# Windowed attention and a gated convolution: band masks by TensorE, gates from SBUF, and a new order

## The chip, the cores and the metric

The kernel runs on one core of a Trainium2 chip. The metric is the device time of one execution in microseconds. Five engines work side by side, each on its own list of instructions in order: TensorE (PE, matmuls, with its weight loads shown as PEld), VectorE (DVE), ScalarE (ACT), GpSimd (POOL), and SyncE (SP), which here does nothing but issue DMAs. The engines wait for each other through semaphores. SBUF is the working memory of 128 partitions; PSUM, eight banks of 128 x 512 float32, takes the results of TensorE.

## The reference

Inputs are q, k, v of shape (8 batches, 8 heads, 576 positions, 64), w_in (512 x 1024), conv_w (3 x 1024) and w_out (1024 x 512), all float32.

```python
scores = np.matmul(q, k.transpose(0, 1, 3, 2)) / np.sqrt(64)
mask = np.abs(pos[:, None] - pos[None, :]) <= 32
attn = softmax(np.where(mask, scores, -1e9))
x = (attn @ v), heads side by side      # (8, 576, 512)
h = np.maximum(x @ w_in, 0.0)           # (8, 576, 1024)
conv = conv_w[0]*h[s-1] + conv_w[1]*h[s] + conv_w[2]*h[s+1]   # along the sequence
out = (h * sigmoid(conv)) @ w_out       # (8, 576, 512)
```

Every query sees only the keys at most 32 positions away, so the attention is a band.

## The kernel before

The program is written out as one list of words, ORDER, some 1,100 steps long. Each word is a step on one engine (`sc,2,1,0@0` is the score block of batch 2, head group 1, part 0, into PSUM bank 0), and every engine runs its instructions in the order in which the words stand. The list was made by a planner that isn't part of the kernel; at run time nothing is decided. Pinned (L159) wraps the engines, so that every instruction shows the one line L165 in the profile and is told apart by its tiles.

**Attention.** A unit is a batch and a group of four heads, 16 units in all. `lq`, `lk` load q and k of a unit into `st` (589,824 bytes each as a whole, or by halves), `cq`, `ck` cast them to bf16 (`qb`) on ACT (a) or POOL (p), `tq`, `tk` transpose 32 x 32 blocks on DVE into `qT`, `kT`. `sc` (L247) makes a score block: for each of four or five tiles of 64 queries it multiplies 128 keys by 64 queries, for four heads, in two halves of the head dimension; the array is used as four row tiles of 32 rows, one head's half each, and each head writes its own PSUM bank. `ex` is the exponential on ACT from PSUM into `attn`. `mk` (L273) multiplies `attn` by a mask on DVE (d), or cuts the two triangles off with two selects on POOL (p). `av` multiplies by v with a column of ones, `nr` divides by the sum into `xn`. v is loaded by `lv` (five blocks of 128 positions a batch, into the single tile `vst`), cast by `cv` into `ve`, and copied shifted by 64 partitions into `vo` by `vo` or by a DMA, `vd`. `xn` is turned into `xT` by a DMA (`xt`) or by TensorE and a copy (`xp`, `xe`).

**The gated convolution.** Two batches make three chunks of 384 positions, twelve chunks in all. The first two are worked as halves of 192, so there are 14 pieces P; 0 to 3 are halves. Each piece has four channel pairs (2 x 128 channels). For each pair: `ph` is the projection, eight matmuls; `re` the relu into `hT` on ACT; `pc` (L448) the convolution into PSUM; `th` (L498) the tanh (the sigmoid is written with it); `ga` (L515) the gate on DVE, (tanh + 1) x h into `gT`; later `py` is the output product, `ye` its copy out of PSUM and `st` the store. The convolution has kinds, chosen word by word:

- P: three matmuls by diagonal matrices for each 128 channels, on the full array.
- D, A: the same on quarters, 64 x 64 tiles, four at a time; the second half of the result then stands with its partitions swapped. Kind D gates with three instructions, the last two over 64 partitions; kind A has its second tanh, in two instructions, put the partitions right and write to `z` in SBUF.
- X: the first tap on ACT, the other two on DVE (`tp`), in PSUM.
- G: all taps on POOL in SBUF (`zg`), tanh from there into PSUM.

All other kinds gate from PSUM. `conv_w` itself is loaded by ACT's queue (`s1`, L607), turned by a matmul (`cw`), copied out (`cc`) and spread into diagonals (`dg`, on ACT or DVE). `id` and `ia` are matmuls whose results nobody reads; they keep TensorE running at the start.

## Time and profile before

| | |
|---|---|
| median of three runs | 211.1 us (210.82 to 212.81) |
| the profiled execution | 212.45 us |
| its span, first to last instruction | 210.7 us |
| TensorE's mean granted clock | 0.992 |
| POOL busy | 147.7 us, 177 instructions |
| DMA traffic | 46.9 MB, 223 GB/s in the mean |
| last output product ends | 207.76 us after the span's start |

The profile lists busy time by engine, by stretches of the span, by groups of equal instructions, and the chain of work that ended last. "Idle before" of a group is the time its engine stood still just ahead of it, and the names behind an arrow tell what ended that wait. Where two instructions of an engine overlap by some tenths, their mean durations add up to more than the busy time.

### The profile page before, as it was taken

The numbers are of one execution on the slowest core, as the hardware profiler recorded it, in microseconds if no ns is written. First come the engines' busy times: TensorE is split into PE (matmuls) and PEld (weight loads), VectorE is DVE, ScalarE is ACT, GpSimd is POOL, SyncE is SP. The second block draws the span as 40 slices with busy tenths as digits, with TensorE's granted clock in tenths as the row PEclk, the third lists the DMA queues.
The fourth block names the chain that finished last, engine by engine and source line by source line (L and its number), as shares of the span: only waits on it lengthen the run. The fifth ranks groups of instructions, "written<-read, shape, count | busy, mean of one in ns | idle before, by whom it ended". The sixth has DMA issues, their size and how long they took to land.

```text
span 210.7 us, 7141 instructions
## 1 busy us (share of the span) xinstructions
PE 195.7 (93%) x2951; PEld 113.9 (54%) x2974; DVE 178.4 (85%) x297; ACT 172.7 (82%) x265; POOL 147.7 (70%) x177
## 2 busy tenths in 40 slices
PE   3867999999999799999999999999999999999994
PEld 2233798895465345654464554554545565555443
DVE  4677977999999998797999779899999587899860
ACT  2986798997999798779999699899978799759911
POOL 2650586499999469999699998539954879955700
PEclk9979999999999999999999999999999999999999
DMA  5999999999998895899999999999976444222225
GB/s 176 325 213 347 388 220 273 366 296 272 318 279 194 195 319 151 267 292 238 241 258 176 226 252 231 262 297 245 290 144 165 99 142 128 46 71 103 100 100 199
DMA packets 66165, 46.90 MB, mean 223 GB/s; under 512 B 53180, under 2 KB 55508, under 8 KB 66132
## 3 DMA queue, kind: packets, MB, share of 16 engines
q1 hardware_dynamic: 66096, 46.43, 84.0%
q8 instruction: 23, 0.38, 0.8%
q14 instruction: 10, 0.08, 0.1%
q10 hardware_dynamic: 36, 0.01, 0.1%
HBM read 32.52 MB, written 9.44 MB: 199 GB/s over the span
## 4 chain that ended last, share of the span: by engine, by line
PE 56%; DVE 16%; DMA 8%; SPq 7%; ACT 6%; issue 5%; ACTq 0%; DVEq 0%
PE PS L165 56%; SPq L165 7%; DVE gT L165 6%; DMA vst<-in_v_dram 6%; DVE xn L165 4%; DVE PS L165 2%; DMA st<-in_q_dram 2%; ACT hT L165 2%; ACT attn L165 1%; ACT PS L165 1%; DVE attn L165 1%; DVE rec L165 1%; ACT y L165 1%; DVE qT L165 1%; DVE kT L165 1%
## 5 line engine op out<-in xcount | busy, mean ns | idle before, releaser
L165 PE MATMUL PS<-xT,w_in_sb 128*128 128x385 bf16 (+3 forms) x448 | 69.5, 305 | 0.5 <-ACT y L165 0.3
L165 PE MATMUL PS<-w_out_sb,gT 128*128 128x512 bf16 (+1 forms) x273 | 64.7, 373 | 1.5 <-issue 0.5
L165 DVE SCALAR_TENSOR_TENSOR gT<-PS,hT 128x384 bf16<-128x384 f32 (+2 forms) x82 | 52.5, 649 | 3.9 <-ACT PS L165 2.9
L165 PEld LDWEIGHTS <-w_in_sb 128*128 128x128 bf16 x448 | 40.6, 98 | 23.1 <-issue 3.2
L165 ACT ACTIVATE hT<-PS 128x770 bf16<-128x770 f32 (+3 forms) x56 | 39.9, 722 | 9.7 <-PE PS L165 7.2
L165 PEld LDWEIGHTS <-gT 128*128 128x128 bf16 x296 | 27.6, 98 | 30.2 <-issue 1.2
L165 ACT ACTIVATE attn<-PS 128x1280 bf16<-128x1280 f32 (+1 forms) x32 | 36.0, 1132 | 4.9 <-PE PS L165 4.5
L165 POOL TENSOR_TENSOR zg<-zg,tap 128x768 f32<-128x768 f32 (+1 forms) x18 | 31.8, 1766 | 1.5
L165 ACT ACTIVATE PS<-PS 128x768 f32<-128x768 f32 (+1 forms) x47 | 29.9, 651 | 3.3 <-PE PS L165 1.9
L165 PE MATMUL PS<-hT,diag_w 64*64 64x384 bf16 (+2 forms) x354 | 27.6, 310 | 0.4 <-ACT hT L165 0.2
L165 DVE TENSOR_TENSOR xn<-PS,rec 128x512 bf16<-128x512 f32 (+1 forms) x32 | 26.4, 825 | 1.1
L165 POOL TENSOR_SCALAR ve<-vst 128x512 bf16<-128x512 f32 x24 | 16.9, 715 | 13.3 <-DMA vst<-in_v_dram 12.8
L165 POOL TENSOR_SCALAR vo<-vst 64x512 bf16<-64x512 f32 x32 | 22.7, 709 | 2.5
L165 DVE TENSOR_TENSOR attn<-attn,mask 128x1280 bf16<-128x1280 bf16 (+1 forms) x24 | 22.5, 942 | 2.2 <-ACT attn L165 2.1
L165 POOL TENSOR_SCALAR qb<-st 128x1152 bf16<-128x1152 f32 (+1 forms) x18 | 18.7, 1043 | 7.4 <-DMA st<-in_q_dram 5.4
L165 POOL TENSOR_SCALAR_AFFINE_SELECT attn<-attn 64x1024 bf16<-64x1024 bf16 (+1 forms) x16 | 19.7, 1233 | 5.3 <-ACT attn L165 4.3
L165 DVE STREAM_TRANSPOSE qT<-qb 128x576 uint32<-128x576 uint32 (+1 forms) x18 | 20.1, 1128 | 3.0 <-POOL qb L165 1.6
L165 DVE STREAM_TRANSPOSE kT<-qb 128x576 uint32<-128x576 uint32 (+1 forms) x18 | 19.9, 1123 | 1.4 <-PE PS L165 0.8
L165 POOL TENSOR_SCALAR tap<-hT,conv_w_sb 128x384 f32<-128x384 bf16 (+1 forms) x36 | 20.1, 571 | 0.9
L165 ACT COPY y<-PS 128x512 f32<-128x512 f32 (+1 forms) x24 | 13.5, 577 | 7.8 <-PE PS L165 7.7
L165 ACT CAST qb<-st 128x1152 bf16<-128x1152 f32 (+1 forms) x18 | 19.1, 1074 | 0.2 <-DVE y L165 0.2
L165 PEld LDWEIGHTS <-diag_w 64*64 64x64 bf16 (+1 forms) x354 | 15.2, 103 | 7.3 <-issue 3.4
(50 smaller groups left out, 205.6 us busy)
## 6 DMA issues: line engine op xcount, KB each, us to landing
out_dram<-y SPq DMA_DIRECT2D x35, 256.0 KB, 3.9
st<-in_k_dram SPq DMA_DIRECT2D x14, 576.0 KB, 6.8
st<-in_q_dram SPq DMA_DIRECT2D x14, 576.0 KB, 6.1
vst<-in_v_dram SPq DMA_DIRECT2D x24, 256.0 KB, 6.8
vst<-in_v_dram SPq DMA_DIRECT2D x16, 192.0 KB, 6.4
st<-in_k_dram SPq DMA_DIRECT2D x4, 288.0 KB, 5.3
st<-in_q_dram SPq DMA_DIRECT2D x4, 288.0 KB, 4.4
vo<-ve SPq DMA_DIRECT2D x8, 130.0 KB, 3.3
```

The costliest lines, as they stand in the source:

```text
L165: return lambda *args, **kwargs: tc.keep_in_program_order(do(*args, **kwargs))
```

## The change

There are no masks any more. `band` is a 128 x 256 matrix that holds -131072 outside a diagonal band; for each head (row tile) and each half of 32 queries `sc` first multiplies a shifted piece of it by the identity, repeated over the block's tiles, into the bank, and the scores are then added there. The exponential makes zeros of what lies outside. `mk`, the full mask and its copy are gone.

Kinds p, x, a and g are added: their tanh goes to SBUF (`z`, or `zg` itself), and one gate instruction reads it there. 32 of the 56 conv pairs use them. `z` has four buffers of two channel tiles each. Half pieces may use the kinds on quarters, each channel tile then in a bank of its own. Of the 40 whole pairs, P, A, D, X, G were used by 5, 7, 13, 7, 8; now P or p 1, A 3, a 11, D 7, X or x 9, G or g 9. Of the 16 half pairs 14 were P, one X, one G; now P 8, p 6, a 1, x 1.

The first q and k of batch 0 are loaded whole (they were halves), and ORDER is a new list. `gq`, `gk`, `gi`, `go` are defined, but no word uses them. By engine, ORDER now has seven casts of whole q and k fewer on ACT and more on POOL, six `vo` steps more on DVE and four fewer on POOL, two diagonals more on DVE and two fewer on ACT. Behind the first score block stood 18 products of `id` and `ia` before the projections, and there are 10 now.

```diff
+MASKED = -131072.0
 ORDER = """
-lk,0,0,0 lq,0,0,0 s3 s1 lq,0,0,1 lk,0,1,1 s2 lk,0,1,0 lk,0,0,1 cw@5 id,7@7 lq,0,1,1 lq,0,1,0 cc lv,0,2 dg,1,a dg,0,d
...
+s3 lq,0,0 cq,0,0,1,a tq,0,0,1 s1 cw@5 id,5@7 ia,0,0,1,1@7 lq,0,1 s4 cc lk,0,0 lv,0,2 lk,0,1 lv,0,1 cq,0,0,0,a
...
-    z_ = tiles(3, [128, CH], FP32, "z")
+    z_ = tiles(4, [128, 2, CH], FP32, "z")
...
-    mask = tiles(1, [128, 4 * 5 * 64], BF16, "mask")[0]
-    mask1 = tiles(1, [128, 64], BF16, "mask1_")[0]
+    band = tiles(1, [128, 256], BF16, "band")[0]
...
+        ts = tiles_of(h)
+        out4 = PS[:, bank:bank + 4, 0:64 * len(ts)].rearrange("p a (t x) -> p a t x", x=64)
+        for i in range(2):
+            for a in range(4):
+                lo = 32 * a
+                tensor.matmul(
+                    out4[:, a, :, 32 * i:32 * i + 32],
+                    band[lo:lo + 32, lo - 32 * i + 32:lo - 32 * i + 160],
+                    ident[lo:lo + 32, None, lo:lo + 32].broadcast_to([32, len(ts), 32]),
+                    start=(i == 0), stop=False, skip_group_check=True,
+                )
+        for t in ts:
             for e in range(2):
                 for a in range(4):
                     tensor.matmul(
                         PS[:, bank + a, 64 * (t - t0):64 * (t - t0) + 64],
                         kT[32 * a:32 * a + 32, 64 * t:64 * t + 128, e],
                         qT[32 * a:32 * a + 32, 64 * t:64 * t + 64, e],
-                        start=(e == 0), stop=(e == 1),
+                        start=False, stop=(e == 1), skip_group_check=True,
                     )
...
-    def mk(b, G, h, e):
-        attn, n = attn_of(b, G, h)
-        if e == "d":
-            vector.tensor_tensor(out=attn, in0=attn, in1=mask[:, 0:4 * n], op=ALU.mult)
-            return
-        for lo, sign in ((0, 1), (64, -1)):
-            part = attn[lo:lo + 64].rearrange("p (t x) -> p t x", x=64)
-            gpsimd.affine_select(
-                out=part, in_=part, compare_op=ALU.is_ge, fill=0.0, base=0,
-                pattern=[[0, n // 16], [-sign, 64]], channel_multiplier=sign,
-            )
...
+    def tanh(to, of):
+        scalar.activation(to, of, AF.Tanh, bias=0.0, scale=1.0)
+
     def th(P, m2, kind, bank=None):
-        if kind == "G":
-            where["pc", P, m2] = bank
-            scalar.activation(
-                conv_out(P, m2), where["zg", P, m2][:, :, 0:width(P)], AF.Tanh, bias=0.0, scale=1.0
-            )
+        w = width(P)
+        if kind in "Gg":
+            zg = where["zg", P, m2][:, :, 0:w]
+            if kind == "G":
+                where["pc", P, m2] = bank
+            tanh(conv_out(P, m2) if kind == "G" else zg, zg)
             return
-        ps = conv_out(P, m2)
-        if kind != "A":
-            scalar.activation(ps, ps, AF.Tanh, bias=0.0, scale=1.0)
+        ps = conv_out(P, m2, kind)
+        if kind in "PDX":
+            tanh(ps, ps)
             return
-        where["z", P, m2] = z = z_[n_z[0] % 3]
+        where["z", P, m2] = z = z_[n_z[0] % 4][:, :, 0:w]
         n_z[0] += 1
-        scalar.activation(ps[:, 0, :], ps[:, 0, :], AF.Tanh, bias=0.0, scale=1.0)
+        if kind in "px":
+            tanh(z, ps)
+            return
+        tanh(ps[:, 0, :] if kind == "A" else z[:, 0, :], ps[:, 0, :])
         for lo in (0, 64):
-            scalar.activation(z[lo:lo + 64, :], ps[64 - lo:128 - lo, 1, :], AF.Tanh, bias=0.0, scale=1.0)
+            tanh(z[lo:lo + 64, 1, :], ps[64 - lo:128 - lo, 1, :])
 
     def ga(P, m2, kind):
...
-        ps = conv_out(P, m2)
+        if kind in "pax":
+            ps = where["z", P, m2]
+        elif kind == "g":
+            ps = where["zg", P, m2][:, :, 0:width(P)]
+        else:
+            ps = conv_out(P, m2, kind)
...
-        vector.memset(mask1, 1.0)
+        vector.memset(band, 0.0)
 
     def s2():
-        for base, sign in ((0, 1), (64, -1)):
+        for base, sign in ((-32, 1), (96, -1)):
             gpsimd.affine_select(
-                out=mask1, in_=mask1, compare_op=ALU.is_ge, fill=0.0, base=base,
-                pattern=[[-sign, 64]], channel_multiplier=sign,
+                out=band, in_=band, compare_op=ALU.is_ge, fill=MASKED, base=base,
+                pattern=[[sign, 256]], channel_multiplier=-sign,
             )
```

How the order moves is seen engine by engine. On SP, the program's first loads before (st are the float32 tiles of q and k, vst those of v, 1152 columns a whole load, x2 two equal rows in turn):

```order
L165 DMA st1_62<-in_k_dram 128x576
L165 DMA st0_61<-in_q_dram 128x576 x2
L165 DMA st3_64<-in_k_dram 128x576 x2
L165 DMA st1_62<-in_k_dram 128x576
L165 DMA st2_63<-in_q_dram 128x576 x2
L165 DMA vst0_77<-in_v_dram 128x8x64 x3
L165 DMA vst0_77<-in_v_dram 96x8x64 x2
L165 DMA st5_66<-in_k_dram 128x1152
```

and now:

```order
L163 DMA st0_61<-in_q_dram 128x1152
L163 DMA st2_63<-in_q_dram 128x1152
L163 DMA st1_62<-in_k_dram 128x1152
L163 DMA vst0_77<-in_v_dram 128x8x64
L163 DMA st3_64<-in_k_dram 128x1152
L163 DMA vst0_77<-in_v_dram 128x8x64
L163 DMA vst0_77<-in_v_dram 96x8x64
L163 DMA vst0_77<-in_v_dram 128x8x64
L163 DMA vst0_77<-in_v_dram 96x8x64
L163 DMA xT1_92<-in_moe_w_in_dram 128x4x256
```

Both q come first, the second unit's k stands behind a load of v, and v's five loads end ninth instead of thirteenth.

On ACT, the program's first rows before (conv_w240 is the tile of the conv weights, attn the result of an exponential, ve the cast v):

```order
L165 DMA conv_w240_116<-in_moe_conv_w_dram 24x128
L165 ACT_TABLE_LOAD
L165 ACTIVATE diag_w0_112<-ident0_113,conv_w_sb0_111 128x128 x3
L165 CAST qb0_67<-st0_61 128x576
L165 ACTIVATE diag_w0_112<-ident0_113,conv_w_sb0_111 128x128 x12
L165 CAST qb3_70<-st3_64 128x576
L165 CAST qb2_69<-st2_63 128x576
L165 ACTIVATE attn1_83<-PS_118 128x1280
L165 ACTIVATE attn0_82<-PS_118 128x1024
L165 ACTIVATE attn3_85<-PS_118 128x1280
L165 CAST ve0_78<-vst0_77 128x8x64 x3
L165 ACTIVATE attn2_84<-PS_118 128x1024
```

and now, up to the first evictions of xT:

```order
L163 CAST qb0_67<-st0_61 128x576
L163 ACTIVATE diag_w0_113<-ident0_114,conv_w_sb0_112 128x128 x6
L163 CAST qb2_69<-st2_63 128x576
L163 CAST qb1_68<-st1_62 128x576
L163 ACTIVATE diag_w0_113<-ident0_114,conv_w_sb0_112 128x128 x3
L163 ACTIVATE attn0_82<-PS_118 128x1024
L163 ACTIVATE attn1_83<-PS_118 128x1280
L163 CAST ve0_78<-vst0_77 128x8x64
L163 ACTIVATE attn2_84<-PS_118 128x1024
L163 ACTIVATE attn3_85<-PS_118 128x1280
L163 CAST ve0_78<-vst0_77 128x8x64
L163 ACTIVATE diag_w0_113<-ident0_114,conv_w_sb0_112 128x128 x3
```

Ahead of the first row shown now stand the table load, one cast of qb0 and the issue of the conv weights' load, in this order. That issue has moved from the first place to behind a cast that waits for q, and the last exponential no longer stands behind three casts of v.

On DVE, in the middle of the program before (gT is written by the gates, attn by the masks):

```order
L165 SCALAR_TENSOR_TENSOR gT_96<-PS,hT_93 128x384
L165 SCALAR_TENSOR_TENSOR gT_96<-PS,hT_93 64x384 x2
L165 SCALAR_TENSOR_TENSOR gT_96<-PS,hT_93 128x768 x2
L165 STREAM_TRANSPOSE kT_75<-qb_70 128x18x32
L165 STREAM_TRANSPOSE kT_74<-qb_68 128x18x32
L165 TENSOR_TENSOR attn_83<-attn_83,mask_114 128x1280
L165 SCALAR_TENSOR_TENSOR gT_96<-PS,hT_93 128x384
L165 SCALAR_TENSOR_TENSOR gT_96<-z_105,hT_93 128x384
```

and now, at the same chunk's gates:

```order
L163 SCALAR_TENSOR_TENSOR gT_96<-PS,hT_93 128x768
L163 SCALAR_TENSOR_TENSOR gT_96<-z_103,hT_93 128x768
L163 STREAM_TRANSPOSE kT_74<-qb_68 128x18x32
L163 STREAM_TRANSPOSE qT_72<-qb_69 128x18x32
L163 SCALAR_TENSOR_TENSOR gT_96<-zg_107,hT_93 128x768
L163 SCALAR_TENSOR_TENSOR gT_96<-PS,hT_93 128x384
L163 SCALAR_TENSOR_TENSOR gT_96<-PS,hT_93 64x384 x2
```

The mask is gone from between them, and two of the four gates read z and zg in SBUF.

200 lines of the change are left out of this document (99 added, 101 removed).

## The prediction

> **What bounds the kernel now.** I read the page's first two parts, then busy time by stretches, the chain that ended last, the timeline of the start, and the groups by form. First the page and the stretches (columns: length; busy us and instructions of PE, PEld, DVE, ACT, POOL; granted clock; DMA share; GB/s):
>
> ```profile
> PE 195.7 (93%) x2951; PEld 113.9 (54%) x2974; DVE 178.4 (85%) x297; ACT 172.7 (82%) x265; POOL 147.7 (70%) x177
> 0.00:5.00 5.00, 1.78 (x6) 0.93 (x7) 1.93 (x13) 0.89 (x1) 1.20 (x8) 1.00 0.56 167
> 5.00:10.00 5.00, 4.52 (x16) 1.65 (x15) 3.06 (x14) 4.99 (x16) 2.96 (x5) 1.00 0.97 329
> 10.00:15.00 5.00, 2.78 (x117) 1.74 (x116) 3.95 (x7) 4.41 (x7) 3.23 (x4) 0.83 0.94 204
> 15.00:20.00 5.00, 4.28 (x60) 1.84 (x58) 3.57 (x10) 3.15 (x6) 0.00 (x0) 0.83 1.06 332
> 24.00:207.50 183.50, 178.91 (x2682) 105.49 (x2702) 162.07 (x248) 155.19 (x232) 139.25 (x159) 1.00 0.85 216
> ```
>
> From 24 us, when the projections begin, to 207.5 us PE is busy 178.91 of 183.50 us. So 4.6 us at most can be won there by freeing other engines, though DVE (162) and ACT (155) are not far behind. The rest of the time is the start: until 24 us PE mostly multiplies fillers. What the start waits for is in the chain (start, length, what) and in the timeline (the same columns, then the count, and in brackets the idle time before and what ended it):
>
> ```profile
> 12.29 6.16 DMA vst<-in_v_dram
> 18.47 0.62 ACT ve L165
> 19.09 0.93 ACT attn L165
> 20.05 0.69 DVE attn L165
> 24.30 0.83 PE L165 MATMUL PS<-xT,w_in_sb 128*128 128x193 bf16 x8
> 27.80 0.84 PE L165 MATMUL PS<-xT,w_in_sb 128*128 128x193 bf16 x8
> 27.45 0.42 PE L165 MATMUL PS<-qT,kT 32*128 32x64 bf16 x32
> 0.81 0.61 ACTq L165 DMA_DIRECT2D conv_w<-in_moe_conv_w_dram  x1
> 3.22 0.58 PE L165 MATMUL PS<-ident,conv_w 24*128 24x24 f32 x2 [3.22 <-DMA conv_w<-in_moe_conv_w_dram]
> 3.84 0.18 DVE L165 COPY conv_w_sb<-PS 128x24 f32<-128x24 f32 x1 [1.58 <-PE PS L165]
> ```
>
> The last load of v lands at 18.45; its cast on ACT holds the last exp behind it, then comes a mask, and the first projection starts at 24.30, the fourth at 27.80.
>
> **The change part by part.** Prices (busy us, mean ns | idle before):
>
> ```profile
> L165 PE MATMUL PS<-qT,kT 32*128 32x64 bf16 x1152 | 15.1, 192 | 2.8 <-ACT attn L165 1.5 <-DVE gT L165 0.6 <-DVE xn L165 0.4
> L165 PE MATMUL PS<-hT,diag_w 64*64 64x384 bf16 x240 | 13.4, 330 | 0.0
> L165 PE MATMUL PS<-hT,diag_w 128*128 128x384 bf16 x30 | 5.6, 326 | 0.2 <-ACT hT L165 0.2
> L165 POOL TENSOR_SCALAR qb<-st 128x576 bf16<-128x576 f32 x5 | 3.3, 673 | 5.1 <-DMA st<-in_q_dram 4.2 <-DMA st<-in_k_dram 0.9
> L165 DVE STREAM_TRANSPOSE qT<-qb 128x288 uint32<-128x288 uint32 x4 | 2.7, 709 | 1.6 <-POOL qb L165 1.6
> L165 ACT ACTIVATE attn<-PS 128x1280 bf16<-128x1280 f32 x16 | 19.8, 1240 | 3.4 <-PE PS L165 3.2
> L165 ACT ACTIVATE attn<-PS 128x1024 bf16<-128x1024 f32 x16 | 16.4, 1025 | 1.5 <-PE PS L165 1.2 <-POOL ve L165 0.3
> L165 ACT CAST xT<-PS 128x512 bf16<-128x512 f32 x9 | 5.0, 592 | 0.0
> L165 ACT ACTIVATE hT<-PS 128x386 bf16<-128x386 f32 x12 | 5.8, 498 | 1.7 <-PE PS L165 1.7
> L165 ACT ACTIVATE diag_w<-ident,conv_w_sb 128x128 bf16<-128x128 bf16 x18 | 5.6, 389 | 0.0
> L165 ACT CAST w_in_sb<-xT 128x1024 bf16<-128x1024 f32 x1 | 1.0, 1045 | 0.3 <-DMA xT<-in_moe_w_in_dram 0.3
> ```
>
> *The start.* Four whole loads take the place of eight halves, and the five loads of v's first batch stand 4th and 6th to 9th on SP, where they were 9th to 13th. Bytes are unchanged. At the first stretch's rate, 167 GB/s, 0.84 MB are in by 5 us, so the first q (0.59 MB) lands between 3.5 and 5; I take 4.4; ACT casts a half (0.67), and only then issues the load of the conv weights, which moves behind that wait on ACT's queue. It took 2.4 us from issue to PE before, so it is there at 7.5; with 0.58 and 0.18 the weights are out at 8.3. Queued behind them on ACT: six diagonals (18 take 5.6, so 1.9) and two half casts (1.3), to 11.5. Transpose 0.7 and a score block 0.4 give the first exp near 12.7. The second unit's k is the fifth load; with 0.84 MB by 5 us, 1.65 more by 10 and then 204 GB/s, its 2.62 MB are in by 10.7. It is cast on POOL as two halves (1.35) and transposed by 13, in time. From there ACT alone sets the pace: four exps 4.5, two v casts 1.2, three diagonals 1.0, a cast of w_in 1.0, two evictions of xT 1.2, together 9.0, less about 0.9 since the instructions overlap by some 0.1 each: 20.8 for the first projection. Before the fourth come one more w_in cast, two relus at 0.5 and three evictions (0.6, 0.6, 0.4), 3.6: 24.4. That is 3.4 earlier than 27.80, with the same two things beside it on PE. For waits that I don't see I take **-2.6**, bounds -4.5 and +1.
>
> *Masks to TensorE.* Each of the 32 score blocks gets eight matmuls, 128 or 160 columns over four banks, ahead of its 32 or 40. The trace has no such matmul. The row with four 32-row tiles gives 13.1 ns for each of 1152 (15.1 us); from the timeline, 32 in 0.42 us less one's own 0.19 is 7.4 ns a piece for 64 columns. By columns, 2 to 2.5 times that, 15 to 18.5 ns, eight make 0.13 us: 4.3 for 32 blocks, **+3.8** for the 28 behind the start. Lower bound: 13.1 each whatever the columns, 0.105 a block, 2.9. Upper: if the four did not run side by side, the row of 384 columns (5.6 / 30 = 187 ns) scaled to 144 is 70 ns, 15.7 us. I take the first, whose row has the same tile shape. No score wait is added on PE beyond the band itself, which POOL writes before the second k is there.
>
> *Conv pairs.* Of whole pairs, 5 on full tiles become 1 and 20 on quarters 21; one half pair more goes to quarters. A full pair is 6 x 5.6/30 = 1.12, a quarter pair 12 x 13.4/240 = 0.67, a half one on quarters about half that. 4 x 1.12 - 0.67 - 0.33 = **-3.5** on PE, bounds -4 and -2.5. So what the bands cost PE, the conv pairs give back.
>
> *The other engines.*
>
> ```profile
> L165 DVE TENSOR_TENSOR attn<-attn,mask 128x1280 bf16<-128x1280 bf16 x13 | 13.8, 1059 | 0.3 <-ACT attn L165 0.3
> L165 DVE TENSOR_TENSOR attn<-attn,mask 128x1024 bf16<-128x1024 bf16 x11 | 8.8, 804 | 1.9 <-ACT attn L165 1.9
> L165 POOL TENSOR_SCALAR_AFFINE_SELECT attn<-attn 64x1024 bf16<-64x1024 bf16 x10 | 11.4, 1142 | 4.8 <-ACT attn L165 4.1 <-DVE gT L165 0.4
> L165 DVE SCALAR_TENSOR_TENSOR gT<-PS,hT 128x384 bf16<-128x384 f32 x36 | 19.3, 549 | 2.1 <-ACT PS L165 2.0
> L165 DVE SCALAR_TENSOR_TENSOR gT<-PS,hT 128x768 bf16<-128x768 f32 x20 | 18.9, 951 | 1.3 <-ACT PS L165 0.9
> L165 DVE SCALAR_TENSOR_TENSOR gT<-z,hT 128x384 bf16<-128x384 f32 x7 | 7.0, 1000 | 0.0
> L165 DVE SCALAR_TENSOR_TENSOR PS<-hT,conv_w_sb,PS 128x384 f32<-128x384 bf16 x28 | 15.4, 616 | 2.2 <-ACT PS L165 2.2
> L165 DVE COPY vo<-ve 64x520 bf16<-64x520 bf16 x16 | 4.7, 291 | 1.7 <-ACT ve L165 1.1 <-POOL ve L165 0.5
> ```
>
> DVE loses masks worth 22.6 and gains two scalar-engine conv pairs (8 x 0.616 = 4.9) and twelve v copies (3.5). POOL loses 16 selects, ten of which took 11.4, and gets seven whole q, k casts from ACT, each about two of the half casts' 0.67. The gates are the doubtful part. Those that read SBUF took 1000 ns where the same size from PSUM took 549, and the timeline says why:
>
> ```profile
> 66.95 1.81 POOL L165 TENSOR_TENSOR zg<-zg,tap 128x768 f32<-128x768 f32 x1
> 67.38 1.80 DVE L165 SCALAR_TENSOR_TENSOR gT<-z,hT 128x384 bf16<-128x384 f32 x1
> 136.59 0.53 DVE L165 SCALAR_TENSOR_TENSOR gT<-z,hT 128x384 bf16<-128x384 f32 x1
> ```
>
> The gate of 67.38 ends 0.42 after POOL's add at 68.76; with POOL idle the same gate took 0.53. So a gate from SBUF waits out the POOL instruction in progress, 1.00 - 0.53 = 0.47 us in the mean of seven. The Trainium skill says why ("SBUF — State Buffer", section "SBUF: two separate sides"): DVE and GpSimd share one port pair, an exclusive lock held for the whole instruction, which a DVE instruction with two SBUF inputs needs against a GpSimd one that reads SBUF. The trace agrees (0.53 alone, 1.80 behind the add), and the rule speaks against this change.
>
> The Trainium skill's rule would leave DVE's sum as I work it out next; without it (a gate from SBUF priced as one from PSUM) that sum would be some 15 us less, and the time the same, since PE bounds either way.
>
> Gates before: 20 pairs x 0.95, 13 on quarters with three at 0.55, 7 at 0.55 + 1.0, 16 half pairs x 0.55: 60.2. After: 6 x 0.95, 7 x 1.65, 3 x 1.55, 24 pairs in one gate from SBUF at 0.95 + 0.47, half pairs 8 x 0.55 and 8 x 1.02: 68.6. So DVE has -22.6 + 4.9 + 3.5 + 8.4 = -5.8, about 173; two diagonals more and an output copy less are left out as small. ACT gets three tanh instructions for one in seven pairs and gives up the seven casts. So no engine but PE is the bound, and I count **0** for waits on the others, bounds -3 (most of the 4.6 idle) and +6.
>
> **Sum.** -2.6 + 3.8 - 3.5 + 0 = -2.3 against the profiled execution's 212.45 (span 210.7 and 1.75 around it): 210.15. The median of the runs is 211.1, 1.35 below the profiled one, so **208.8**.
>
> **Rivals.**
> - *The gates' port (the slower side).* In-order PE stands behind late gates. Place: the output product that follows the last gate of a chunk, 14 chunks or half chunks. It decides once a gate lands later than PE arrives there; PE idles only 4.6 us in 183.5 now, so it arrives early. One wait of 0.47 at each of 12 of them is +5.6: **214.4**. Today (us in total, times, longest):
>
> ```profile
> PE PS L165 <- DVE gT L165: 0.8, 2, 0.6
> PEld L165 <- DVE gT L165: 1.7, 4, 0.4
> ```
>
>   For it: the mean wait above and 32 such gates. Against: DVE has about 6 us more room, and PSUM banks come free after the tanh, not after the gate.
> - *The start is given back.* The conv weights land late among the q and k loads (nothing in the trace shows that load under traffic), or PE's clock falls as the work begins. In 10 to 20 us it was granted 0.83, which is half speed for 2 x 5 x 0.17 / 0.5 = 3.4 us, after a stretch with 2.78 of 5 us busy; 18 filler products came behind the first scores then, 10 do now. Half speed over the first 3.4 us of projections costs 1.7. The Trainium skill's rule on it ("TensorE: Matmul & The Clock Gate", section "What's actually happening") is that a window of about 3.4 us with little work halves the clock until one with enough; the row fits. Without the start's gain: **211.4**; with the clock as well, 213.
> - *More than that.* The start comes at its worked 3.4 and PE closes 2.5 of its 4.6 idle us because no mask stands between exp and product any more: **205.5**.
> - *Bands one after another.* If the row tiles don't overlap with this moving pattern: 15.7 for 3.8, **220.7**. Against: the score matmuls with the same tiles do overlap.
>
> **How the numbers follow.** Forecast, 207 to 210.2: 0.30. The start given back, 210.2 to 213.2: 0.25. Faster still: 0.22. Port: 0.17. Bands serial: 0.06. A measurement of this kernel tells 1% from nothing, so faster means below 209.0 and slower above 213.2. Of the forecast's case about two thirds is below 209.0: with the rival on that side 0.43 (0.20 + 0.22, rounded). Slower: port and bands 0.23, a little of the second rival, less what of the port's case is milder: 0.25. The rest, 0.32, is within 1%. The range takes in the port and leaves out serial bands and the far ends: 204 to 215.
>
> **What would show it.** The first projection before 22 us and the fourth before 26 (start). Band matmuls with a score block of about 0.5 instead of 0.35 to 0.42 us (bands). Full-tile conv rows of 384 columns six instead of 30 (pairs). Gates from z and zg with means of 1.2 to 1.5 us at 768 elements, and PE waiting for "DVE gT" more than those 0.8 and 1.7 us (port). I am wrong if the score blocks take over 0.8 us, if the granted clock is below 1.0 after the first projection, or if DVE's sum rises instead of falling.

## The result, and the profile after

The changed kernel takes **221.8 us** in the median of four runs (220.2 to 222.4), against 211.5 us for the kernel before beside it: a ratio of **1.047, with a 95% interval of 1.039 to 1.054**. It is some 10 us slower, and 6.8 us above the upper end of the predicted range. Ratios, here and below, are formed from undisturbed runs beside the kernel before on the same chip, so they need not be the quotient of two medians.

First the page's busy line of the changed kernel, and its stretches, cut as for the kernel before: the start, and from the first projection to the last product (length; busy us and instructions of PE, PEld, DVE, ACT, POOL; granted clock; DMA share; GB/s).

```profile
PE 194.1 (88%) x3198; PEld 115.9 (53%) x3223; DVE 173.3 (79%) x277; ACT 171.8 (78%) x272; POOL 138.3 (63%) x161
0.00:5.00 5.00, 0.00 (x0) 0.00 (x0) 0.57 (x8) 1.88 (x2) 0.71 (x6) 1.00 0.63 224
5.00:10.00 5.00, 0.00 (x0) 0.00 (x0) 1.13 (x9) 0.72 (x2) 2.81 (x6) 1.00 1.08 343
28.80:217.30 188.50, 179.14 (x2923) 108.05 (x2941) 161.02 (x239) 156.90 (x246) 121.25 (x133) 1.00 0.76 200
```

PE, DVE, ACT and POOL are each busy for less time than before, and the program is longer. Two places take it. Until 10 us PE does nothing at all, and ACT and DVE hardly anything. And behind the first projection PE is busy for 179.14 us, 0.2 more than before, but in a stretch of 188.5 us: it stands idle for 9.4 us where it was 4.6.

The timeline of the start shows what PE waits for (start, length, engine, what, count; in brackets the idle time before and its cause):

```profile
4.41 0.60 ACTq L163 DMA_DIRECT2D conv_w<-in_moe_conv_w_dram  x1
10.32 0.59 PE L163 MATMUL PS<-ident,conv_w 24*128 24x24 f32 x2 [10.32 <-DMA conv_w<-in_moe_conv_w_dram]
10.95 0.18 DVE L163 COPY conv_w_sb<-PS 128x24 f32<-128x24 f32 x1 [4.71 <-PE PS L163]
11.23 1.86 ACT L163 ACTIVATE diag_w<-ident,conv_w_sb 128x128 bf16<-128x128 bf16 x6 [5.51 <-DVE hT L163]
18.35 0.29 PE L163 MATMUL PS<-ident,band 32*128 32x128 bf16 x8
18.48 0.41 PE L163 MATMUL PS<-qT,kT 32*128 32x64 bf16 x32
29.08 1.78 PE L163 MATMUL PS<-xT,w_in_sb 128*128 128x193 bf16 x16
32.27 3.56 PE L163 MATMUL PS<-xT,w_in_sb 128*128 128x193 bf16 x40
```

The conv weights are issued at 4.41, behind the first cast, and reach PE at 10.32. Three engines stand in line for them, since the program order of each has a step that needs them: PE's `cw`, DVE's `cc` (4.71 us idle, with the transposes of q and k behind it), ACT's diagonals (5.51 idle, with casts of q and k behind them). From `cw` to 18.35 PE works through 21 filler products, so the first scores start at 18.48, and the first projection at 29.08, 4.8 us later than in the profile before; the fourth is the second of the run of 40 matmuls at 32.27, near 32.9 instead of 27.80.

The groups by form (busy us, mean ns | idle before) of DVE, and the one full-tile convolution group that the prediction named:

```profile
L163 DVE SCALAR_TENSOR_TENSOR gT<-z,hT 128x768 bf16<-128x768 f32 x17 | 19.5, 1153 | 0.0
L163 DVE COPY vo<-ve 64x520 bf16<-64x520 bf16 x28 | 17.2, 613 | 4.7 <-ACT ve L163 4.1
L163 DVE SCALAR_TENSOR_TENSOR gT<-zg,hT 128x768 bf16<-128x768 f32 x7 | 7.6, 1084 | 0.9 <-ACT zg L163 0.9
L163 PE MATMUL PS<-hT,diag_w 128*128 128x384 bf16 x6 | 1.1, 327 | 0.0
```

A gate of 768 elements from SBUF costs 0.13 to 0.20 us more than from PSUM (950 ns), not 0.47. The vo copies cost 613 ns where they cost 291 before.

Last, the later stretch: a line of the timeline, three of the table of waits (engine, what it waited for: us in total, times, longest), and the page's DMA rate in its 40 slices of 5.5 us:

```profile
45.28 0.22 PE L163 MATMUL PS<-ve,attn 128*64 128x65 bf16 x1 [2.24 <-issue]
PE PS L163 <- DVE kT L163: 2.2, 2, 1.4
PE PS L163 <- DVE gT L163: 0.4, 1, 0.4
SPq L163 <- ACT qb L163: 15.1, 1, 15.1
GB/s 236 320 269 395 270 252 383 286 292 220 0 113 156 296 156 226 346 142 254 195 365 206 163 237 293 235 310 297 106 277 223 167 74 59 52 106 103 48 179 154
```

PE does not wait for gates: 0.4 us, against 0.8 before. It stands still for 2.24 us in the middle of a block with nothing late that the profile shows (the last section comes back to it), and it waits for kT. SP, which issues every load of q, k and v in order, stands for 15.1 us at one load whose buffer ACT hasn't cast yet, and the DMA engines run out of work: the eleventh slice, from 55 to 61 us, has 0 GB/s. What each of these three costs is worked out under e1.

### The profile page after: what moved, and what is told of

The parts are those of the page before. It is cut to its first block, busy times and chain, and to the rows that moved or that the text cites. A ratio compares the mean times of both kernels' runs of the same rounds, so it can differ in the third digit from the quotient of the medians.

```text
span 220.6 us, 7590 instructions
## 1 busy us (share of the span) xinstructions
PE 194.1 (88%) x3198; PEld 115.9 (53%) x3223; DVE 173.3 (79%) x277; ACT 171.8 (78%) x272; POOL 138.3 (63%) x161
## 4 chain that ended last, share of the span: by engine, by line
PE 59%; DVE 18%; ACT 8%; DMA 7%; issue 5%; SPq 2%; DVEq 0%; ACTq 0%
PE PS L163 59%; DVE gT L163 7%; DVE vo L163 3%; DMA conv_w<-in_moe_conv_w_dram 3%; DMA xT<-xn 2%; ACT attn L163 2%; DVE xn L163 2%; SPq L163 2%; ACT hT L163 2%; DVE kT L163 2%; DVE qT L163 2%; DMA st<-in_q_dram 2%; ACT PS L163 1%; ACT xT L163 1%; DVE y L163 1%
## 5 line engine op out<-in xcount | busy, mean ns | idle before, releaser
L163 ACT ACTIVATE hT<-PS 128x770 bf16<-128x770 f32 (+3 forms) x56 | 40.1, 724 | 11.0 <-PE PS L163 10.6
L163 ACT ACTIVATE attn<-PS 128x1024 bf16<-128x1024 f32 (+1 forms) x32 | 36.0, 1130 | 14.2 <-PE PS L163 14.1
L163 POOL TENSOR_TENSOR zg<-zg,tap 128x768 f32<-128x768 f32 x18 | 33.6, 1869 | 1.5
L163 ACT ACTIVATE z<-PS 64x384 f32<-64x384 f32 (+4 forms) x55 | 28.2, 514 | 1.5 <-PE PS L163 0.9
L163 DVE SCALAR_TENSOR_TENSOR gT<-z,hT 128x768 bf16<-128x768 f32 (+1 forms) x28 | 28.0, 1009 | 0.3 <-ACT z L163 0.2
L163 POOL TENSOR_SCALAR zg<-hT,conv_w_sb 128x384 f32<-128x384 bf16 x18 | 12.5, 706 | 23.4 <-ACT hT L163 23.3
L163 DVE SCALAR_TENSOR_TENSOR PS<-hT,conv_w_sb,PS 128x384 f32<-128x384 bf16 (+1 forms) x40 | 21.4, 597 | 7.0 <-ACT PS L163 6.9
L163 DVE SCALAR_TENSOR_TENSOR gT<-PS,hT 128x384 bf16<-128x384 f32 (+2 forms) x38 | 23.2, 614 | 3.5 <-ACT PS L163 2.9
L163 POOL TENSOR_SCALAR ve<-vst 128x512 bf16<-128x512 f32 x25 | 17.6, 713 | 12.5 <-DMA vst<-in_v_dram 6.6
L163 PE MATMUL PS<-hT,diag_w 64*64 64x384 bf16 (+3 forms) x354 | 24.1, 306 | 0.8 <-DVE gT L163 0.4
L163 POOL TENSOR_SCALAR tap<-hT,conv_w_sb 128x384 f32<-128x384 bf16 x36 | 23.3, 660 | 0.6
L163 DVE COPY vo<-ve 64x520 bf16<-64x520 bf16 x28 | 17.2, 613 | 4.7 <-ACT ve L163 4.1
```

The lines of the kernel that those rows point to most:

```text
L163: return lambda *args, **kwargs: tc.keep_in_program_order(do(*args, **kwargs))
```

## The experiments

All ratios are to the kernel before. "First projection" is its start in the one profiled run, in us, and can be off where that run was; the us in the third column are the ratio's difference times 211.1.

| run | ratio (95% interval) | us | first projection |
|---|---|---|---|
| kernel before | 1 | 0 | 24.30 |
| changed kernel | 1.047 (1.039 to 1.054) | +9.9 | 29.08 |
| e1: conv weights first | 1.000 (0.995 to 1.005) | 0.0 | 21.10 |
| e2: no fillers | 1.048 (1.037 to 1.059) | +10.1 | 25.38 |
| e3: both | 1.010 (0.999 to 1.021) | +2.1 | 20.15 |
| e5: conv weights as fourth load | 1.048 (1.041 to 1.056) | +10.2 | 27.47 |
| e10: before, weights late | 1.034 (1.025 to 1.042) | +7.1 | 33.50 |
| e4: before, with bands | 1.018 (1.009 to 1.026) | +3.7 | 22.54 |
| e6: e1 without bands | 0.997 (0.993 to 1.001) | -0.6 | 20.38 |
| e11: before, SBUF gates | 1.022 (1.018 to 1.025) | +4.5 | 22.90 |
| e12: before, bands and SBUF gates | 1.032 (1.025 to 1.038) | +6.6 | 22.28 |
| e7: e1, gates back to PSUM | 1.026 (1.019 to 1.034) | not used | |
| e8: e1, vo copies by POOL | 1.051 (1.046 to 1.057) | +10.9 | 22.07 |
| e9: e1, vo copies from float32 | 1.028 (1.023 to 1.032) | +5.8 | 20.41 |
| e13: before, start moved | 1.003 (1.000 to 1.006) | +0.6 | 23.34 |
| e14: e13 with D for A | 1.015 (1.010 to 1.020) | +3.2 | 23.20 |

The theory after the two profiles was that the late conv weights and the fillers behind them make the start late, and that the rest of the loss follows from it; the rivals were DVE's port, and a start whose time is given back whatever is done to it.

### e1: the conv weights' load first

```diff
-s3 lq,0,0 cq,0,0,1,a tq,0,0,1 s1 cw@5 id,5@7 ...
+s3 s1 lq,0,0 cq,0,0,1,a tq,0,0,1 cw@5 id,5@7 ...
```

> The changed kernel with one word moved: the load of the conv weights is issued by ACT before its first cast of q, not behind it. Theory A (those weights land at 10.2 us among the loads of q, k and v, and hold DVE's transposes, ACT's diagonals and PE's fillers behind them): the load is issued near 1 us and lands before 5, the first projection moves from 29.07 to 23 to 25 us, and the time falls by 4 to 6 us, to 216 to 218. Rival B (the start is paced by the loads of q, k and v and by ACT, whatever the weights do): the first projection stays within 1 us of 29, and the time at 221 to 222. Rival C (time won at the start is given back later, since DVE and the loads pace the middle): the first projection moves early, but the time falls by less than 2 us.

One word is moved, and the whole loss is gone: some 10 us, for the 4 to 6 that theory A had said. From the timeline of e1, its stretch from the first projection to the last product, and SP's wait:

```profile
2.85 0.58 PE L163 MATMUL PS<-ident,conv_w 24*128 24x24 f32 x2 [2.85 <-DMA conv_w<-in_moe_conv_w_dram]
10.67 0.41 PE L163 MATMUL PS<-qT,kT 32*128 32x64 bf16 x32
21.10 1.51 PE L163 MATMUL PS<-xT,w_in_sb 128*128 128x193 bf16 x16
24.33 3.56 PE L163 MATMUL PS<-xT,w_in_sb 128*128 128x193 bf16 x40
20.90:204.40 183.50, 180.31 (x2944) 108.21 (x2936) 156.45 (x239) 156.49 (x245) 127.16 (x140) 1.00 0.84 217
SPq L163 <- ACT qb L163: 3.6, 1, 3.6
```

Issued at 0.74, the weights reach PE at 2.85. Scores and first projection come 8 us earlier. PE's idle time behind the first projection falls from 9.4 to 3.2 us, and SP's one long wait from 15.1 to 3.6. (This profiled run took 209.4 us, 2.5 less than the median of e1's ten runs, 211.9.)

Both kernels run the same list on every engine but for that one word, so their profiles can be laid beside each other row by row. At the fourth projection (32.9 and 24.9) the changed kernel is 8 us late. Four rows of it from the time of SP's wait and after, and then two of e1, the same cast and the same two gates:

```profile
61.70 1.19 ACT L163 CAST qb<-st 128x1152 bf16<-128x1152 f32 x1
62.94 2.63 DVE L163 SCALAR_TENSOR_TENSOR gT<-z,hT 128x384 bf16<-128x384 f32 x2
62.96 2.20 POOL L163 TENSOR_TENSOR zg<-zg,tap 128x768 f32<-128x768 f32 x1
68.71 0.48 PE L163 MATMUL PS<-qT,kT 32*128 32x64 bf16 x40 [0.75 <-DVE kT L163]
```

```profile
51.40 1.18 ACT L163 CAST qb<-st 128x1152 bf16<-128x1152 f32 x1
52.64 1.00 DVE L163 SCALAR_TENSOR_TENSOR gT<-z,hT 128x384 bf16<-128x384 f32 x2
```

PE's 2.24 us of standing still bring the delay from 8 to 10.3 us. It is still 10.3 at the cast of 61.70, which ends SP's wait: so that wait comes of the delay, and nothing was lost while it lasted. Then DVE falls behind. Two gates from z take it 2.63 us beside POOL's add, where e1 takes 1.00, and PE waits 0.75 us for the kT that DVE transposes behind them. Two gates of 768 elements (2.77 us for 1.93) and two vo copies (1.68 for 0.82), both beside POOL's casts, do the same until 99 us, and the three steps add 0.7, 0.8 and 0.7 us to the delay. From there it changes by no more than 0.6 us, and at the end it is 12.9. So between these two executions the late start cost more than itself: 8 us at the start, 2.2 in PE's stall, and 2.2 where DVE's instructions now meet POOL's. (The ratios, from all runs, put the whole at 9.9.)

### e2 and e3: without the fillers

e2 is the changed kernel without the 21 products of `id` and `ia` between `cw` and the first scores; e3 is e1 and e2 together.

```diff
-... cw@5 id,5@7 ia,0,0,1,1@7 lq,0,1 ... ia,0,0,0,3@7 lv,0,0 ... ia,0,1,0,3@7 s5 ... ia,0,1,1,5@7 ia,1,0,0,4@7 ck,0,0,1,a
+... cw@5 lq,0,1 ... lv,0,0 ... s5 ... ck,0,0,1,a
```

> The changed kernel without the 21 products of id and ia that stand on PE between the turn of the conv weights and the first score block; their results are read by nobody. Theory A: they held the first score block from about 15 to 18.35 us, so it starts near 15 and the first projection near 26 instead of 29.07; the time falls by 2 to 3 us, to 219 to 220. Rival B (the fillers only fill waits): the first score block stays near 18, the time at 221 to 222. Rival C (without them PE's clock is granted at half speed when the score blocks and projections begin): the granted clock between 15 and 35 us falls below 0.9, and the time rises to 223 to 225.

> Both of these edits: the conv weights' load issued first, and no fillers before the first score block. Theory A: first projection near 22 to 23 us, time 214 to 216 (7 us below the changed kernel); what then remains above the kernel before, 3 to 5 us, was lost behind the fourth projection. If the start explains all of the loss, 211 to 212. Rival C (given back later): 218 or more.

From the timeline of e2, its first scores:

```profile
15.20 0.61 PE L163 MATMUL PS<-qT,kT 32*128 32x64 bf16 x32 [3.91 <-DVE kT L163]
```

Theory A was right on the start (15.2, then 25.38, in place of 18.48 and 29.08), and rival B fell with that. Rival C fell too: the granted clock was 1.00 from 15 to 35 us. On the time the record does not decide. By the ratios none of the 3.7 us reached the end, but e2's interval goes from 7.7 to 12.5 us. The median of its four runs, 219.9 us, lies in theory A's range, and in the two profiles 2.9 of the 3.7 us are left at the end (spans of 217.7 and 220.6 us). So the fillers may have cost some 3 us or nothing; they are not the cause of the 10. In e3 the first scores came at 10.45, hardly sooner than in e1 with its fillers (10.67), since there PE waits for POOL to write the band:

```profile
PE PS L163 <- POOL band L163: 6.5, 1, 6.5
```

e3 is 2.1 us above the kernel before, from two runs alone, with an interval from 0 to 4.5; at 214.2 us in the median it fits theory A's 214 to 216, but e1, with the fillers, is no slower, so that reading is gone. Between e2 and e3 only the place of the load differs: 8.0 us, by their ratios and by the spans of their profiles (217.7 and 209.7) alike.

### e5: the conv weights as the fourth load

```diff
-s3 lq,0,0 cq,0,0,1,a tq,0,0,1 s1 cw@5 id,5@7 ia,0,0,1,1@7 lq,0,1 s4 cc lk,0,0 lv,0,2 ...
+s3 lq,0,0 cq,0,0,1,a tq,0,0,1 lq,0,1 lk,0,0 s1 cw@5 id,5@7 ia,0,0,1,1@7 s4 cc lv,0,2 ...
-        scalar.dma_start(conv_w24, ...
+        sync.dma_start(conv_w24, ...
```

> The changed kernel, with the conv weights' load issued by SP as its fourth load, behind the two first q and the first k (1.77 MB), not by ACT. Theory A (a load lands when the bytes issued before it have landed): in the run with the load issued first, 1.135 MB were moved by 5 us and then 340 GB/s, so 1.77 MB are in near 6.9 us and the weights reach PE at 6.5 to 7.5 us, against 2.85 issued first and 10.3 in the changed kernel; the first projection falls between theirs, at 22.5 to 25 us, and the time is 213 to 217. Rival B (a small load gets its share whatever is ahead of it; it was only issued late): the weights are there by 5 us, the first projection near 21, the time near 212.

```profile
7.59 0.59 PE L163 MATMUL PS<-ident,conv_w 24*128 24x24 f32 x2 [7.59 <-DMA conv_w<-in_moe_conv_w_dram]
15.80 0.41 PE L163 MATMUL PS<-qT,kT 32*128 32x64 bf16 x32
22.71 0.22 PE L163 MATMUL PS<-vo,attn 128*64 128x65 bf16 x1 [1.99 <-issue]
27.47 2.77 PE L163 MATMUL PS<-xT,w_in_sb 128*128 128x193 bf16 x16
25.00:30.00 5.00, 4.94 (x72) 4.50 (x72) 2.95 (x6) 2.51 (x4) 3.86 (x5) 0.50 0.93 218
```

The 12 KB arrive at 7.6, just past the range that theory A worked out from the 1.77 MB ahead of them, and far from rival B's 5: a small load lands when the bytes issued before it have. The same count fits the changed kernel: by 4.41 SP had issued four loads of q and k and one of v, 2.6 MB, and 224 and 343 GB/s over the first two stretches move 2.8 MB by 10 us. In the changed kernel the weights even had a queue of their own (ACT's), and still their packets ran only from 8.29 to 9.61. The rest of the expectation fell. The scores start some 8 us after `cw`, as in the changed kernel and in e1, but the first projection comes 11.7 later, not 10.4 to 10.6. Two things of this execution take its lead away: PE stands for 1.99 us at 22.71, released by nothing in the profile (the last section comes back to it), and the granted clock is 0.50 from 25 to 30 us (the last row above). Its fourth projection comes at 32.7, as in the changed kernel (32.9). Of its four runs the two at a clock of 1.00 took 219.7 and 219.8 us, the two at 0.98 took 222.7 (the profiled one) and 222.9. So e5 shows where the weights land; what a start some 2.7 us earlier is worth it does not show.

### e10: the same word in the kernel before

```diff
-lk,0,0,0 lq,0,0,0 s3 s1 lq,0,0,1 ...
+lk,0,0,0 lq,0,0,0 s3 cq,0,0,0,a s1 lq,0,0,1 ...
-lv,0,1 dg,2,d cq,0,0,0,a ia,0,0,0,1@7 ...
+lv,0,1 dg,2,d ia,0,0,0,1@7 ...
```

> The kernel before with one cast of q (cq,0,0,0,a) moved ahead of the load of the conv weights on ACT's queue, nothing else: what the change does to that load, done to the old order. Theory A (the late load by itself makes the loss): the load is issued near 4 us and the weights land at 8 to 10.5 us instead of 3.22, the first projection moves from 24.3 to 28 to 31, and the time rises by 4 to 8 us, to 215 to 219. Rival B (the old order, whose loads are halves and whose scores don't wait for 21 fillers, takes it up): less than 2 us slower, 213 or less.

```profile
9.92 0.59 PE L165 MATMUL PS<-ident,conv_w 24*128 24x24 f32 x2 [9.92 <-DMA conv_w<-in_moe_conv_w_dram]
```

With one cast ahead of the load, the weights come at 9.92 in place of 3.22, and the old kernel loses 7.1 us (5.3 to 8.8), with no band and no new gate in it. Theory A holds on the landing and on the time. The profiled run has its first projection at 33.50, later than the 28 to 31 said, but it took 220.4 us, 2.6 more than the mean of the two runs of the ratio, with a granted clock of 0.64 and 0.68 between 25 and 35 us. Undone in the new order and done in the old one, the late load is shown to be the cause of most of the 10 us.

### e4 and e6: the bands alone, in the old order and in the new

e4 is the kernel before with the band matmuls of the changed one in `sc`, and `mk`, `s7` and the mask tiles gone. e6 is e1 without the band matmuls.

```diff
 (e4) +        for i in range(2):
      +            for a in range(4):
      +                tensor.matmul(out4[:, a, :, 32 * i:32 * i + 32], band[...], ident[...], start=(i == 0), ...)
      -mk,0,0,1,d ... (32 words)
 (e6) -        for i in range(2): ... (the same eight matmuls)
```

> The kernel before, in its own order, with the one part of the change that puts the bands on PE: eight matmuls ahead of each score block, no masks on DVE or POOL, nothing else. Theory A (the band costs PE what was priced, 0.13 us a block, and frees DVE of 22.6 us and POOL of 16 selects): PE busy rises by 4 to 5 us, DVE's busy sum falls to about 156, POOL's to about 130; PE bounds, so the time is 0 to 3.5 us above the kernel before, 211 to 215. Rival B (the waits for masks were on the path and go): 208 to 211. Rival C (bands disturb the score blocks or the order more than their price, and carry the loss by themselves): 217 or more.

> The kernel with the conv weights' load issued first, without the eight band matmuls of each score block: the masking is left out. It prices the bands in the new order. Theory A (PE bounds, the bands cost what was priced): 3 to 4.5 us less than with them, 207.5 to 209. Rival B (PE has slack there, something else bounds): within 1 us of 211.9. Rival C (bands cost more than their own duration, since they also part the score blocks from their weight loads): 206 or less.

The busy lines of e4 and of e6, and two of e6's waits on PE:

```profile
PE 200.6 (95%) x3230; PEld 117.3 (55%) x3230; DVE 155.0 (73%) x272; ACT 173.7 (82%) x265; POOL 122.1 (58%) x161
```

```profile
PE 193.1 (92%) x2967; PEld 112.7 (54%) x2967; DVE 169.7 (81%) x277; ACT 171.5 (82%) x272; POOL 137.3 (66%) x161
PE PS L163 <- DMA xT<-xn: 2.3, 1, 2.3
PE PS L163 <- DVE xn L163: 2.1, 4, 0.8
```

In the old order bands cost 3.7 us (2.0 to 5.5), where the prediction had priced PE's part at 3.8: theory A. That DVE gets 23 us of room and POOL 26 buys nothing. In the new order theory A fell and rival B held: without its bands e1 is only 0.6 us faster than the kernel before (from 1.5 faster to 0.3 slower), where 3 to 4.5 were expected. PE has 2.4 us less to do than in e1 (195.5) and waits longer instead, for xT and xn. So there PE is not what bounds.

### e11 and e12: the gates from SBUF, in the old order

e11 is the kernel before with the tanh of the same number of pairs, 32, written to SBUF; e12 has the bands of e4 besides.

```diff
+        if kind == "G":
+            tanh(zg, zg)
...
+        tanh(z, ps)          # A, X and eight half pairs of P; z has four buffers [128, 2, CH]
...
+            ps = where["z", P, m2]
+        gate(gT[:, m:m + 2, :], ps, taps(P, (m, m + 1), 1))
```

> The kernel before, in its own order and with its masks, with only the tanh of 32 pairs (all of A, X and G, eight half pairs of P) written to SBUF and gated from there in one instruction. Theory A (the wait behind POOL is 0.2 to 0.25 us for a gate, on an engine with room): DVE's busy sum changes by less than 5 us, the time stays within 2 us of the kernel before. Rival B (the gates' port, as the prediction's first rival had it): 3 to 6 us slower, with PE waiting for DVE gT. Rival C (banks that come free after the tanh and not after the gate let PE go ahead): 1 to 3 us faster.

> The kernel before, in its own order, with both parts that can be put into it alone: the bands on PE in place of the masks, and the tanh of the same 32 pairs to SBUF with their gates there. Alone they cost 1.76% (3.7 us) and 2.15% (4.5 us). Theory A (both lengthen the same in-order chain, so they add): 218 to 220.5, 7 to 9 us above the kernel before; the new order with its early weights, at 0.0%, has then won some 8 us back by its start, its conv pairs and its order. Rival B (the bands' relief of DVE and POOL takes up the gates' waits): 213 to 216, no more than the larger of the two. Rival C (masks and gates fought for the same port, and both go): below 213.

A group of POOL in the kernel before, and then in e11 the same and the busy line:

```profile
L165 POOL TENSOR_SCALAR tap<-hT,conv_w_sb 128x384 f32<-128x384 bf16 x32 | 18.4, 589 | 0.8
```

```profile
L165 POOL TENSOR_SCALAR tap<-hT,conv_w_sb 128x384 f32<-128x384 bf16 x32 | 22.8, 724 | 0.8
PE 198.4 (93%) x2974; PEld 113.6 (53%) x2974; DVE 181.8 (85%) x290; ACT 173.2 (81%) x265; POOL 159.2 (75%) x177
```

The gates cost 4.5 us (3.8 to 5.3): rival B's size. That PE would wait for gT, as rival B had it, does not show: it waited 0.6 us for it. Where the 4.5 us arise stays open. What the rows show is that both engines are longer, DVE by 3.4 us and POOL, with the same 177 instructions, by 11.5. Bands and gates together cost 6.6 us (5.2 to 8.1). That is more than either and less than the 8.2 of the two, a sum that is itself known to some 2 us, so they add for the most part: between theory A and rival B, and rival C is out. With the weights early the new order stands at 0.0, so its start, its fewer conv pairs on PE and its other steps are together worth about as much as bands and gates cost; which of them is worth how much was not measured apart.

### e7, e8, e9: gates and vo copies in the new order

e7 is e1 with the letters a, p, x of 25 pairs written as A, P, X. e8 lets POOL make the 28 vo copies of DVE. e9 lets DVE make them from the float32 tile.

```diff
 (e7) -pc,0,3,p@2 ... th,0,3,p ... ga,0,3,p
      +pc,0,3,P@2 ... th,0,3,P ... ga,0,3,P
 (e8) -vo,0,1,d ... (14 words)
      +vo,0,1,q     # gpsimd, the same tile ve
 (e9) -                copy(e, vo[p0:p0 + 64, c], ve[p1:p1 + 64, cc])
      +                copy(e, vo[p0:p0 + 64, c, :, 0:64], vst[p1:p1 + 64, cc])
```

> The kernel with the conv weights' load issued first, with 25 of its 32 pairs whose tanh goes to SBUF (kinds a, p, x) put back to the kinds that write it to PSUM (A, P, X); the seven of kind g stay. Gates of 384 and 768 elements then read PSUM, which took 549 and 949 ns against 590 and 1065 from z. Theory A (the SBUF gates' waits are small and beside the path): DVE's busy sum falls by 1 to 3 us, the time stays within 1.5 us of 211.9. Rival B (the gates' waits behind POOL hold PE): 2 us or more faster, 210 or less. Rival C (PSUM banks, now held until the gate, come free late): 2 us or more slower, 214 or more.

> The kernel with the conv weights' load issued first, with the 14 steps of vo that DVE did (28 copies from ve, mean 519 ns there, 290 where POOL was idle) done by POOL from the same tile. Theory A (the copies' waits behind POOL are beside the path, since DVE has room): DVE's busy sum falls by some 14 us, the time stays within 2 us of 211.9, or rises where POOL's own queue is late with the first v. Rival B (DVE's lost time at these copies holds the last 2 to 3 us that the forecast is missed by): 209.5 or less.

> The kernel with the conv weights' load issued first; DVE's 28 vo copies now read vst (float32, as POOL's own vo copies do) and not ve, so they need not wait for the cast of v. Theory A (a bf16 copy between SBUF tiles waits out POOL's instruction, one from float32 need not): their mean falls from 519 ns to 300 to 400 with no long ones behind POOL, PE's wait for DVE vo at 16.3 us (1.0) goes, the first projection moves from 21.1 to about 20, the time falls by 0 to 1.5 us from 211.9. Rival B (every DVE copy within SBUF waits for POOL, whatever its type): the mean stays at 500 ns or more, the time within 1 us of 211.9.

e7 decides nothing: in that order 17 of the 25 banks are filled by a later step between tanh and gate, so its gates read other data there and wait for other steps than a working kernel's would. It shows only that the new order counts on banks that are free after the tanh. e8 is 10.9 us above the kernel before, with PE waiting for the copies:

```profile
PE PS L163 <- POOL vo L163: 8.9, 4, 3.4
```

So DVE's long copies are the cheaper choice and rival B fell. Theory A had allowed for a late first v alone, and gave no price: the two longest of these waits, 3.4 and 3.1 us, are at later batches, at 84 and 128 us. In e9 theory A fell but for the first projection (group of DVE, wait of SP):

```profile
L163 DVE CAST vo<-vst 64x512 bf16<-64x512 f32 x28 | 20.0, 715 | 0.5
SPq L163 <- DVE vo L163: 12.2, 3, 7.0
```

A copy from float32 is long beside POOL too (715 ns in the mean, 424 where POOL was idle, against 519 and 291 from bf16 in e1), and now the loads of v wait for DVE. Its first projection is 0.7 us earlier than e1's and its time 5.8 us worse.

### e13 and e14: two attempts to beat both kernels

```diff
 (e13) -... lk,1,0 ex,0,1,1 ... li,1 vo,0,1,d li,3 ... cv,0,4,a ... cv,0,0,a lq,1,1 ex,0,1,0 vo,0,0,d ... mk,0,1,0,d lv,1,2 ck,1,0,a ...
       +... ex,0,1,1 ... li,1 vo,0,1,d li,3 lk,1,0 ... ex,0,1,0 cv,0,4,a ... mk,0,1,0,d ... cv,0,0,a lq,1,1 vo,0,0,d ... xe,0,0,a ck,1,0,a ...
 (e14) -pc,4,1,A@2 ... th,4,1,A ... ga,4,1,A      (7 pairs)
       +pc,4,1,D@2 ... th,4,1,D ... ga,4,1,D
```

> The kernel before with six words of its start moved: the last exp of batch 0 ahead of two casts of v and its mask ahead of a vo copy; the two quarters of w_in that the first projection needs ahead of the next k on SP; that k's cast behind the two evictions of xT; a diagonal ahead of a cast. In the kernel before, the quarter needed by the first projection landed at 22.88 and was cast by 23.95. Theory A (what comes earlier at the start comes out of the time): first projection at 22 to 23 in place of 24.30, time 1 to 2 us less, 209 to 210.3. Rival B (the loads and the other engines pace what follows, and a start won is given back): first projection at 22 to 23, time within 0.5% of 211.1.

> The same start, and the seven pairs of kind A made kind D: one tanh in PSUM in place of three instructions, three gates from PSUM in place of one from PSUM and one from SBUF (1000 ns in the mean there, 530 with POOL idle). No gate reads SBUF any more. Theory A (gates from SBUF cost time by the port they share with POOL; 32 of them cost 4.5 us): about 1 us less than without this edit, 208 to 209.5. Rival B (seven are too few, or DVE's two gates over 64 partitions at 555 ns each take as much): the same within 0.5%.

Neither does. e13 is at 1.003, and does not test its theory: its first projection at 23.34 is earlier than the 24.30 of the profile before, but e11, with the same words at its start, begins at 22.90, so the profiled run of the kernel before was itself late there by some 1.4 us, and nothing was won. ACT's eviction, which was to come earlier, still waits for PE:

```profile
21.85 1.07 ACT L165 CAST xT<-PS 128x512 bf16<-128x512 f32 x2 [1.76 <-PE PS L165]
```

e14 is 2.6 us slower than e13 by their ratios, although ACT has 3.7 us less to do (168.9 of 172.6 busy): theory A fell. Fewer gates from SBUF are no gain by themselves, at least not where kind D takes their place, with its two gates more over 64 partitions and its PSUM banks held until the gate; these were not parted. No working kernel of this study is faster than the kernel before; e1 equals it.

## Why the prediction was wrong, point by point

**The start (-2.6, bounds -4.5 and +1): wrong, and it carries the error.** The step that failed is "It took 2.4 us from issue to PE before, so it is there at 7.5". That 2.4 was of a load issued at 0.81, ahead of all others; issued at 4.41, behind 2.6 MB, it took 5.9. The prediction had the bytes and their rate in the same paragraph, and used them for k but not for the weights. The next step failed as well: it queued only ACT's work behind the weights, while DVE's transposes and 21 fillers on PE stood behind them too. The first projection came at 29.08, not 20.8. With the weights early, e1 has it at 21.10 and the fourth near 24.9, where 20.8 and 24.4 were worked out. That agreement is in part luck, of two errors that cancel: its first exp came at 11.15, not 12.7, since the weights were there at 2.85 and not at 7.5, and the stretch from there to the first projection took 10.0 us, not 8.1. And a start as forecast did not bring the forecast time: e1 stands at 1.000 of the kernel before, where 208.8 would have been 0.989. These 2.3 us (1.2 to 3.4) no run explains.

**The second rival named the cause and mispriced it.** "The conv weights land late among the q and k loads" was there with a chance, but as a gain that doesn't come, at 211.4. Its price was never worked out from what queues behind the weights; e10 puts it at 7.1 us in the old order, e1 at about 10 in the new.

**Waits on other engines (0, bounds -3 and +6): inside the bounds, the value wrong.** PE's idle time behind the first projection rose by 4.8 us, from 4.6 to 9.4. In e1 it is 3.2, so the rise comes with the late start. Of the 6.2 us between the two, 2.24 are PE's stall and 1.6 the longer waits for kT (2.2 for 0.6), which come from DVE meeting POOL.

**Bands (+3.8) and conv pairs (-3.5): the sum is right on PE.** PE's busy time behind the first projection rose by 0.2 us where 0.3 was said (each of the two profiles lacks some 25 matmul records, so 0.2 is rough). The bands ran side by side (eight in 0.29 us), which refutes the fourth rival; alone in the old order they cost 3.7. But the step "PE bounds either way" does not carry to the new order: there e6 takes them away and nothing comes of it. The pairs were not run alone; the busy sums of the convolution's matmul groups fall from 27.7 to 24.0 us, 3.7 where 3.5 was said.

**The gates' port: size about right in the old order, place wrong.** The rival said 5.6 us; e11 measured 4.5 in the old order. The product behind a late gate, where it was to show, is not where PE waits (0.4 us). In the loss of the changed kernel the port has a small part: two of the three places where DVE fell behind POOL, 1.5 us in all, are gates from z, and there PE waits for kT. But e1 undoes the whole loss with all 32 gates in place.

**DVE's sum (about 173): right by luck, of two errors that cancel.** It is 173.3. The gates came to 58.8 us, not 68.6, because a gate waits 0.2 us and not 0.47; and the 28 vo copies to 17.2, not 8.1. The twelve added copies were priced at the 291 ns of the profile before, where no copy had begun behind a POOL instruction. The timelines of DVE, POOL and PE in the changed kernel show the difference:

```profile
21.65 2.98 DVE L163 COPY vo<-ve 64x520 bf16<-64x520 bf16 x4 [4.14 <-ACT ve L163]
21.57 1.15 POOL L163 TENSOR_SCALAR qb<-st 128x1152 bf16<-128x1152 f32 x1 [0.43 <-DMA st<-in_q_dram]
22.99 1.19 POOL L163 TENSOR_SCALAR qb<-st 128x1152 bf16<-128x1152 f32 x1 [0.27 <-DMA st<-in_k_dram]
24.68 0.19 PE L163 MATMUL PS<-vo,attn 128*64 128x65 bf16 x1 [1.57 <-DVE vo L163]
```

Four copies of 0.29 take 2.98 us beside POOL's casts of q and k, and PE waits 1.57 us for the last. The Trainium skill ("SBUF — State Buffer", section "SBUF: two separate sides") says that a DVE instruction in a two-port performance mode takes the same lock as one with two SBUF inputs; the trace agrees (613 ns against 291), and the prediction had applied that page to the gates alone.

**Clock.** The granted clock was 1.00 in every stretch shown, as the forecast took it.

## What to carry to other kernels

A small load that several engines stand in line for is issued first, ahead of anything that its queue could wait for: here it landed when the bytes issued before it had moved, not after the 2.4 us that it took when it was first. When a step is moved, follow every engine whose program order has a step behind it, and don't let a rival that names a cause keep a price of zero. In a program with a fixed order a delay also changes which instructions of two engines meet: 8 us at the start became 12.9 at the end between two profiles. And an early first projection by itself says little of the end: e4, e11 and e12 begin 1.4 to 2.0 us before the profile of the kernel before, and take 3.7 to 6.6 us longer.
